# Causal decay attention and two MoE layers on one core: row maxima carried as ten columns

## The chip, the core and the metric

The kernel runs on one core of a Trainium2 chip. The core has five engines with a queue of instructions each: PE (TensorE, the matmuls), DVE (VectorE), ACT (ScalarE), POOL (GpSimd) and SP (SyncE, which here only issues DMAs). Every queue runs in order, so an instruction that waits holds up all that stands behind it. The metric is the device time of one launch in microseconds; less is better.

## What is computed

```python
# 4 batches, 8 heads, 576 positions, 64 per head; all fp32 (weights arrive as float64 and are converted)
scores = q @ k.T / 8 + cum[:, :, :, None] - cum[:, :, None, :]     # cum = cumsum(log(clip(f, 1e-4, 1)))
scores = where(causal, -1e9, scores)
scores = scores - max(scores, axis=-1, keepdims=True)
attn = exp(scores); attn = attn / (sum(attn) + 1e-9)
x = (attn @ v)                                  # 2304 tokens x 512
h = x @ w_in;  x = (max(h, 0) + alpha * min(h, 0)) @ w_out          # 512 -> 2048 -> 512
h = x @ w_in2; out = (h * tanh(softplus(h))) @ w_out2               # 512 -> 2048 -> 512
```

## The kernel before

**Order.** The program is not written in the order in which it runs. Each step is handed to a planner (class `Plan`) with an engine, a cost, a due time `at` and the keys that it reads and writes. The planner lists the steps for every engine by due time and by what is ready in its own estimate, and each engine then runs its list in order. Two tables bend this: `PRIO` adds an offset to the due time of a step, named by stage and number, and `ENG` says which engine takes a step that several could take.

**Attention.** The 32 heads go in 16 pairs, one head on partitions 0 to 63 and one on 64 to 127. A pair passes these stages. `load_qk` and `load_v` bring q, k and v (SP). `load_bias` brings three rows of the decay to KM (for the maxima) and to BK (for the scores); they come from a tensor `biasd`, which the prologue works out from f, and for pair 0 straight from the prologue's tile. `stage_T` casts q and k to QM and KM on ACT. `stage_M` computes the scores once in a single pass, twelve matmuls per pair into the three banks of the group "one" (banks 4 to 6), and one DVE instruction for each (line 623) takes the maxima along keys; they land in the tile M5. Stage `NM2` at its end turns the maxima into rows: M5 holds five chunks of 128 columns, in which two columns carry maxima and the rest is zero, five PE transpositions (line 635) bring them to a bank pair of the group "two" (banks 0 to 3), and two ACT instructions (line 640) copy the result, with a vector `bvec` that adds the constant rows, to BQ. `stage_S` then computes the exact scores in four pieces, each as q times k plus BQ times BK (line 660), and ACT takes the exponential into Pt. POOL masks the diagonal (line 678) and adds up key blocks (line 696). `stage_R` sums over keys on PE (line 708), and ACT and DVE work out the reciprocal in `rr` and `uu`, of which there is one tile each. `stage_V` multiplies Pt by v (line 742), and DVE scales the result by `uu` into X (line 748).

**Keeping PE warm.** Thirty matmuls with the identity run first (line 519), and four follow each matmul of pair 0's `stage_M` and each piece of its `stage_S`. An fp32 matmul shows as two instructions in the trace.

**MoE layers.** Weights come as float64 and are turned to fp32 in halves, by one ACT instruction (line 399) and three DVE ones (lines 401, 403, 405), and then split into a high part (ACT) and a low part (POOL or DVE, line 331). The first four slots of the first layer, eight tiles, are loaded during pairs 0 to 3. `group_a` runs those four slots for three token blocks as a filler between attention's matmuls, and for the other three blocks after attention (`swap1` frees its memory then). `moe_block` runs the rest: `h_mm` (lines 786 to 788), `prelu` or `mish`, `split_g` (high part on ACT, low part by line 331), `out1` (lines 851 to 853) or `out2` (lines 862 to 864). `store_w` converts the second layer's weights during the first and parks them in DRAM.

Of the kernel before, what the change touches and what calls it, by code (L numbers as in the profile page):

```python
# [237 lines left out]
def fox_attention__then__moe_prelu__then__moe_mish(  # L238
# [282 lines left out]
    def prologue():  # L521
# [60 lines left out]
    def load_v(pr, at):  # L582
        plan.stage("LV2")
        i = pr % 2
        n4 = (NQ - 1) * P
        dma(at, lambda: nc.sync.dma_start(vt[i][:, :NQ - 1], v[pr, :n4].rearrange("(c p) x -> p c x", p=P)), 262, runs=1.3, w=[("v", i, 0)])
        dma(at, lambda: nc.sync.dma_start(vt[i][:HALF, NQ - 1], v[pr, n4:]), 33, r=[("vpad", i)], w=[("v", i, 1)], issue=0.62)
# [454 lines left out]
```

## Time and profile before

| | |
|---|---|
| three runs, median (lowest to highest) | 1057.97 us (1057.28 to 1059.17) |
| the profiled execution, its own time | 1058.0 us |
| span of the profile of that execution | 1056.2 us |
| PE busy | 1017.5 us, 96% of the span |
| DVE, ACT, POOL busy | 745.1, 542.1 and 414.2 us |
| granted TensorE clock, mean | 0.994 |
| DMA | 71.06 MB, mean 67 GB/s |

The span is that of the one profiled execution, and 1.8 us of its time lie outside it. The stages follow each other: attention with its filler to about 277 us, the rest of `group_a` to about 360, the first MoE layer to about 620, and the second to the end. A matmul's busy time overlaps that of its neighbours, so a busy PE need not be a PE at its full rate: the count of matmuls in a stretch tells more.

### The profile page before, as it was taken

Reading aid. Unit: us, or ns where it says so; the run is one execution under the profiler, and the core shown is the slowest. Engines: PE = TensorE matmul, PEld = TensorE weight load, DVE = VectorE, ACT = ScalarE, POOL = GpSimd, SP = SyncE. Lnnn points to the kernel's source line nnn. Section 1 sums busy time; section 2 is a strip of 40 time slices with the busy share of each in tenths; the row PEclk is TensorE's granted clock in tenths of the full one; section 3 lists DMA queues with packets and bytes.
Section 4 is the critical chain, followed back from the end, with each engine's and each line's share of the span. In section 5 each row is a group of like instructions: output and inputs, shape, how many; then the busy total and the mean of one; then the engine's idle time right before and its main releaser. Section 6 shows DMA issues by size and latency. Waiting matters only on the chain.

```text
span 1056.2 us, 16992 instructions
## 1 busy us (share of the span) xinstructions
PE 1017.5 (96%) x5996; PEld 914.7 (87%) x5996; DVE 745.1 (71%) x1673; ACT 542.1 (51%) x1133; POOL 414.2 (39%) x423
## 2 busy tenths in 40 slices
PE   7989999999978999999999999999999999999998
PEld 7756677777778999999999999998999989999897
DVE  6587655656588767888612247979888788887885
ACT  4777656664454544444332336555455454554543
POOL 4575543553455562413232324242233322423231
PEclk9999999999999999999999999999999999999999
DMA  5233221210133345565500034100000000000000
GB/s 163 89 110 98 79 70 36 71 48 12 44 117 100 125 137 183 183 207 182 163 1 1 20 92 129 41 1 31 1 6 25 1 30 1 1 31 1 31 1 31
DMA packets 55399, 71.06 MB, mean 67 GB/s; under 512 B 6673, under 2 KB 32273, under 8 KB 55313
## 3 DMA queue, kind: packets, MB, share of 16 engines
q1 hardware_dynamic: 55312, 69.97, 21.2%
q8 instruction: 47, 0.77, 0.3%
q14 instruction: 40, 0.32, 0.1%
HBM read 56.60 MB, written 13.33 MB: 66 GB/s over the span
## 4 chain that ended last, share of the span: by engine, by line
PE 85%; DVE 6%; DMA 3%; ACT 2%; issue 2%; POOL 1%; SPq 0%; ACTq 0%; DVEq 0%; POOLq 0%
PE b L786 12%; PE b L787 11%; PE b L788 11%; PE b L660 6%; PE b L863 6%; PE b L862 6%; PE b L864 6%; PE b L851 5%; PE b L853 5%; PE b L852 5%; PE b L742 4%; PE b L616 3%; PE b L519 2%; DVE wb L403 2%; PE b L708 2%
## 5 line engine op out<-in xcount | busy, mean ns | idle before, releaser
L786 PE MATMUL b<-xh,w 128*128 128x384 f32 x768 | 261.1, 340 | 9.0 <-ACT x L321 5.4
L788 PE MATMUL b<-xl,w 128*128 128x384 f32 x768 | 258.7, 337 | 0.0
L787 PE MATMUL b<-xh,w 128*128 128x384 f32 x768 | 258.6, 337 | 0.0
L843 POOL TENSOR_TENSOR x<-x 128x384 f32<-128x384 f32 x96 | 112.5, 1172 | 246.6 <-DVE x L841 165.7
L786 PEld LDWEIGHTS b<-xh,w 128*128 128x128 f32 x768 | 145.2, 189 | 17.6 <-ACT x L321 6.4
L787 PEld LDWEIGHTS b<-xh,w 128*128 128x128 f32 x768 | 145.2, 189 | 4.0
L788 PEld LDWEIGHTS b<-xl,w 128*128 128x128 f32 x768 | 145.0, 189 | 0.0
L331 POOL TENSOR_TENSOR g<-X,g 128x384 fp32r<-128x384 f32 x72 | 78.6, 1095 | 164.8 <-ACT g L321 128.4
L851 PE MATMUL b<-g,w 128*128 128x384 f32 x384 | 131.8, 343 | 9.4 <-DVE x L811 2.5
L853 PE MATMUL b<-g,w 128*128 128x384 f32 x384 | 129.8, 338 | 0.7 <-POOL g L331 0.6
L852 PE MATMUL b<-g,w 128*128 128x384 f32 x384 | 129.3, 337 | 0.0
L321 ACT CAST g<-x 128x384 fp32r<-128x384 f32 x120 | 61.4, 512 | 115.5 <-POOL x L843 105.0
L864 PE MATMUL b<-w,g 128*128 128x512 f32 x288 | 113.2, 393 | 0.0
L863 PE MATMUL b<-w,g 128*128 128x512 f32 x288 | 113.2, 393 | 0.0
L862 PE MATMUL b<-w,g 128*128 128x512 f32 x288 | 113.1, 393 | 0.0
L811 DVE SCALAR_TENSOR_TENSOR X<-X,alph,b 128x384 f32<-128x384 f32 x72 | 43.9, 611 | 84.3 <-ACT X L805 83.8
L623 DVE CUSTOM_DVE_ANT_0 junk<-b,tri 128x320 f32<-128x320 f32 (+3 forms) x160 | 69.4, 434 | 45.8 <-PE b L616 33.2
L331 DVE TENSOR_TENSOR g<-x,g 128x384 fp32r<-128x384 f32 x102 | 74.9, 736 | 17.6 <-ACT g L321 17.3
L399 ACT ACTIVATE wb<-raw 128x256 f32<-128x256 f32 x128 | 52.2, 432 | 66.8 <-DMA wd<-wb 38.2
L851 PEld LDWEIGHTS b<-g,w 128*128 128x128 f32 x384 | 72.6, 189 | 13.8 <-DVE x L814 3.4
L805 ACT ACTIVATE X<-b 128x384 f32<-128x384 f32 x72 | 35.2, 489 | 88.7 <-PE b L788 88.0
L401 DVE TENSOR_SCALAR wb<-wb 128x256 int32<-128x256 int32 x128 | 55.1, 450 | 33.9 <-ACT wb L399 33.0
(93 smaller groups left out, 1973.7 us busy)
## 6 DMA issues: line engine op xcount, KB each, us to landing
raw<-in_moe_w_in_dram SPq DMA_DIRECT2D x64, 256.0 KB
raw<-in_moe_w_out_dram SPq DMA_DIRECT2D x64, 256.0 KB
wd<-wb SPq DMA_DIRECT2D x32, 256.0 KB
raw<-wd SPq DMA_DIRECT2D x32, 256.0 KB
qt<-in_q_dram SPq DMA_DIRECT2D x16, 288.0 KB
kt<-in_k_dram SPq DMA_DIRECT2D x16, 288.0 KB
out_dram<-x SPq DMA_DIRECT2D x18, 256.0 KB
vt<-in_v_dram SPq DMA_DIRECT2D x16, 256.0 KB
```

What stands on the lines that cost most here:

```text
L331: plan.add(engs, 0.0, at, lambda e: (nc.gpsimd if e == "POOL" else nc.vector).tensor_tensor(out=out(), in0=in0(), in1=in1(), op=ALU.subtra ...
L623: nc.vector.tensor_tensor_reduce(out=junk[ql, :z - a], in0=ps()[ql, :z - a], in1=tri[ql, x0 + a:x0 + z], scale=-1.0, scalar=BIG if n == 0 ...
L786: nc.tensor.matmul(ps[:, :NB], w[:, 0, c], xh[c], start=(c == 0), stop=False)
L787: nc.tensor.matmul(ps[:, :NB], w[:, 1, c], xh[c], start=False, stop=False)
L788: nc.tensor.matmul(ps[:, :NB], w[:, 0, c], xl[c], start=False, stop=(c == KC - 1))
L843: add("POOL", c_pool(NB, 2.2), lambda e, m: nc.gpsimd.tensor_tensor(out=m, in0=e, in1=m, op=ALU.mult), [ek, mk], [mk])
L851: nc.tensor.matmul(ps[:, :NB], w[:, 0, c], g[:, 0], start=first, stop=False)
L852: nc.tensor.matmul(ps[:, :NB], w[:, 1, c], g[:, 0], start=False, stop=False)
L853: nc.tensor.matmul(ps[:, :NB], w[:, 0, c], g[:, 1], start=False, stop=last)
L862: nc.tensor.matmul(ps, g[:, 0, sl], w[:, 0], start=first, stop=False)
L863: nc.tensor.matmul(ps, g[:, 0, sl], w[:, 1], start=False, stop=False)
L864: nc.tensor.matmul(ps, g[:, 1, sl], w[:, 0], start=False, stop=last)
```

## The change

1. **Maxima.** M5 becomes a tile of 128 x 10, one column for each head and chunk. One PE transposition into one bank of the group "one" gives 10 x 128, one copy (ACT by the tables) brings it to a new tile MT, and four DMAs on SP carry the rows of MT to the two rows of BQ. The constant rows of BQ are written once, in the prologue, by POOL. `bvec` goes.
2. **Loads.** v of pair 0 waits for the bias rows of KM. The first weights are loaded for pairs 1 to 4 in place of 0 to 3, all four `w_in` before the four `w_out`, and each load waits for one of the pair's BQ rows (`behind`).
3. **Two buffers** of `rr` and `uu`; the sums of `stage_R` no longer wait for the last use of `uu`.
4. **Tables.** Nearly every offset of `PRIO` is another, and `ENG` has more entries. Against the list of before, 72 subtractions of `split_g` in the first MoE layer go from POOL to DVE, and six copies out of PSUM go from ACT to DVE on balance. All other instructions stay on their engines. Three DVE steps of the prologue are marked `port=BOTH`, which makes the planner keep them clear of POOL's steps in its own estimate. The diff below leaves `PRIO` out, a line of some 2,000 characters; `ENG` is whole.

```diff
-ENG = {('A0g', 0): 'ACT', ('A1g', 0): 'ACT', ('A2g', 3): 'DVE', ('AX', 1): 'DVE', ('AX', 3): 'DVE', ('AX', 5): 'DVE', ('AX', 7): 'DVE', ('B3', 4): 'DVE', ('H0', 4): 'ACT', ('H1', 14): 'DVE', ('O1', 5): 'DVE', ('WF', 2): 'DVE', ('X0', 1): 'POOL', ('X0', 3): 'POOL', ('X0', 7): 'POOL', ('X1', 3): 'POOL', ('X1', 5): 'POOL', ('X1', 7): 'POOL'}
+ENG = {('A0g', 0): 'ACT', ('A0g', 2): 'ACT', ('A0g', 3): 'POOL', ('A1g', 0): 'ACT', ('A2g', 0): 'DVE', ('A2g', 2): 'ACT', ('A2g', 3): 'DVE', ('A3g', 0): 'DVE', ('AX', 1): 'DVE', ('AX', 2): 'ACT', ('AX', 3): 'DVE', ('AX', 4): 'ACT', ('AX', 5): 'DVE', ('AX', 7): 'DVE', ('B0', 4): 'DVE', ('B3', 4): 'DVE', ('H0', 4): 'ACT', ('H0', 7): 'DVE', ('H1', 13): 'ACT', ('H1', 14): 'DVE', ('NM2', 1): 'ACT', ('NM2', 2): 'ACT', ('O1', 3): 'DVE', ('O1', 5): 'ACT', ('R2', 3): 'POOL', ('T2', 2): 'ACT', ('T2', 3): 'ACT', ('WA', 12): 'ACT', ('WA', 13): 'POOL', ('WF', 2): 'DVE', ('X0', 0): 'ACT', ('X0', 1): 'POOL', ('X0', 2): 'ACT', ('X0', 3): 'POOL', ('X0', 4): 'ACT', ('X0', 6): 'ACT', ('X0', 7): 'POOL', ('X1', 0): 'ACT', ('X1', 3): 'POOL', ('X1', 4): 'ACT', ('X1', 5): 'POOL', ('X1', 6): 'ACT', ('X1', 7): 'POOL'}
...
-            half_w(src, kind, fc, i, m, at, after if i else ())
+            half_w(src, kind, fc, i, m, at, [*(after if i else ()), *behind])
...
+    FIRST = [("KMr", 0, e) for e in range(2)]
+    W_FROM = 1
...
-    M5 = [ap1.tile([P, NQ, P], F32, tag=f"M5{i}", name=f"M5{i}") for i in range(2)]
+    M5 = [ap1.tile([P, 2, NQ], F32, tag=f"M5{i}", name=f"M5{i}") for i in range(2)]
+    MT = [ap1.tile([2 * NQ, P], F32R, tag=f"MT{i}", name=f"MT{i}") for i in range(2)]
...
-    rr = ap1.tile([P, S], F32, tag="rr", name="rr")
-    uu = ap1.tile([P, S], F32, tag="uu", name="uu")
+    rrs, uus = ([ap1.tile([P, S], F32, tag=f"{t}{i}", name=f"{t}{i}") for i in range(2)] for t in ("rr", "uu"))
...
-            plan.add("POOL", 0.7, -17 + 9 * i, lambda i=i: G.memset(M5[i], 0.0), w=[("M5", i, c, e) for c in range(NQ) for e in range(2)])
+            plan.add("POOL", 1.2, -17 + 9 * i, lambda i=i: (
+                G.memset(BQ[i].bitcast(F32), 0.0), [G.memset(BQ[i][e * HALF:e * HALF + 3].bitcast(F32), 1.0) for e in range(2)]), w=[("BQ1", i)])
+            plan.add("POOL", 0.2, -17 + 9 * i, lambda i=i: G.memset(M5[i], 0.0), w=[("M5", i, c, e) for c in range(NQ) for e in range(2)])
...
-        ps, bk = plan.use("two")
-        def tr():
-            for c in range(NQ):
-                q0 = rows(c)[0]
-                half = int(q0 >= W0)
-                nc.tensor.transpose(ps()[half][:, q0 - half * W0:q0 - half * W0 + P], M5[i][:, c], ident)
...
-                    nc.scalar.activation(BQ[i][:, a:z], ps()[half][:, :z - a], AF.Identity, bias=bvec)
...
+        ps, bk = plan.use("one")
+        plan.add("PE", 0.11, at + 6, lambda: nc.tensor.transpose(ps()[:2 * NQ, :P], M5[i].rearrange("p e c -> p (e c)"), ident),
+                 ["ident"] + [("M5", i, c, e) for c in range(NQ) for e in range(2)], [bk, ("MT", i)])
+        copy(at + 6.3, P, lambda: MT[i], lambda: ps()[:2 * NQ, :P], [bk], [("MT", i)], ps=True)
+        for e in range(2):
+            for c, n in ((0, 1), (1, NQ - 1)):
+                q0, w = rows(c)
+                dma(at + 6.5, lambda e=e, c=c, n=n, q0=q0, w=w: nc.sync.dma_start(
+                    BQ[i][e * HALF + 1:e * HALF + 2, q0:q0 + n * w].bitcast(F32),
+                    MT[i][e * NQ + c:e * NQ + c + n, :w].bitcast(F32)),
+                    2, r=[("MT", i), ("BQ1", i)], w=[("BQ", i, e, min(c, 1))], issue=0.62)
...
-                if h < 2 * GA:
-                    load_w(0, h % 2, h // 2, h // 2, at + (h % 2) * II + W_AT)
+                h -= 2 * W_FROM
+                if 0 <= h < 2 * GA:
+                    load_w(0, h // GA, h % GA, h % GA, at + (h % 2) * II + W_AT, behind=[("BQ", pr % 2, 0, 0)])
```

**Where the order moves.** First PE, at the place where pair 0's maxima are turned (tile M50) and its scores begin (line 660, tile BQ0); KM1 and QM1 are pair 1, the second use of KM0 and QM0 is pair 2. Before:

```order
L635 MATMUL b0_65<-ident_73,M50_142 128x128 x3
L635 MATMUL b1_66<-ident_73,M50_142 128x128 x2
L616 MATMUL b4_69<-KM1_1_137,QM1_1_133 128x256
L616 MATMUL b5_70<-KM1_0_136,QM1_0_132 128x64
L616 MATMUL b6_71<-KM1_1_137,QM1_1_133 128x64
L660 MATMUL b2_67<-qt0_124,kt0_127 128x288
L660 MATMUL b3_68<-qt0_124,kt0_127 128x288
L660 MATMUL b2_67<-BQ0_140,BK0_138 128x288
```

And now:

```order
L634 MATMUL b4_69<-ident_73,M50_142 10x128
L620 MATMUL b5_70<-KM1_1_137,QM1_1_133 128x256
L620 MATMUL b4_69<-KM1_0_136,QM1_0_132 128x64
L620 MATMUL b6_71<-KM1_1_137,QM1_1_133 128x64
L620 MATMUL b5_70<-KM1_0_136,QM1_0_132 128x448
L620 MATMUL b4_69<-KM1_1_137,QM1_1_133 128x448
L620 MATMUL b6_71<-KM1_0_136,QM1_0_132 128x320
L620 MATMUL b5_70<-KM1_1_137,QM1_1_133 128x320
L620 MATMUL b4_69<-KM1_0_136,QM1_0_132 128x192
L620 MATMUL b6_71<-KM1_1_137,QM1_1_133 128x192
L620 MATMUL b5_70<-KM0_0_134,QM0_0_130 128x320
L620 MATMUL b4_69<-KM0_1_135,QM0_1_131 128x320
```

Three matmuls stood between the transpositions and the first scores; now eleven do, and pair 1's `stage_M` ends before the scores of pair 0 begin (their rows follow).

Second PE, at the turn of pair 2's maxima (M50 again) and its first scores (qt2, kt2, BQ0). Before, one matmul stands between:

```order
L635 MATMUL b2_67<-ident_73,M50_142 128x128 x3
L635 MATMUL b3_68<-ident_73,M50_142 128x128 x2
L616 MATMUL b4_69<-KM1_0_136,QM1_0_132 128x256
L660 MATMUL b2_67<-qt2_126,kt2_129 128x288
L660 MATMUL b3_68<-qt2_126,kt2_129 128x288
```

And now (L708 is `stage_R` and L743 is `stage_V` of pair 0):

```order
L634 MATMUL b6_71<-ident_73,M50_142 10x128
L620 MATMUL b5_70<-KM1_0_136,QM1_0_132 128x320
L708 MATMUL b0_65<-Pt0_122,ones_157 64x128 x2
L708 MATMUL b0_65<-accp_149,ones_157 64x160 x2
L708 MATMUL b1_66<-accp_149,ones_157 64x288 x2
L743 MATMUL b6_71<-Pt0_122,vt0_147 64x320 x6
L743 MATMUL b6_71<-Pt0_122,vt0_147 64x192 x2
L743 MATMUL b6_71<-Pt0_122,vt0_147 64x64 x2
L620 MATMUL b5_70<-KM1_1_137,QM1_1_133 128x320
L620 MATMUL b4_69<-KM1_0_136,QM1_0_132 128x256
L660 MATMUL b2_67<-qt2_126,kt2_129 128x448
L660 MATMUL b3_68<-qt2_126,kt2_129 128x448
```

The sums over keys, a window of `stage_V` and three matmuls of `stage_M` have moved in between.

Third, after attention, the copy of block 3's output out of bank 4 (tile x2_3), which the next block's first matmuls need. Before it is on ACT, behind the conversions of two weights:

```order
L399 ACTIVATE wb0_92<-raw0_91 128x256 x2
L321 CAST w6_0_2651<-wb0_92 128x512
L399 ACTIVATE wb1_2643<-raw1_2642 128x256 x2
L399 ACTIVATE wb0_92<-raw0_91 128x256 x2
L321 COPY x2_3_2639<-b4_69 128x384
```

Now it is on DVE, after the split of the next block's x:

```order
L403 SCALAR_TENSOR_TENSOR wb1_2633<-raw1_2632,wb1_2633 128x256
L405 SCALAR_TENSOR_TENSOR wb1_2633<-raw1_2632,wb1_2633 128x256 x2
L331 TENSOR_TENSOR xl1_101<-X_111,xh1_97 128x384
L331 TENSOR_TENSOR xl2_102<-X_111,xh2_98 128x384
L323 COPY x2_3_2629<-b4_69 128x384
L331 TENSOR_TENSOR xl3_103<-X_111,xh3_99 128x384
```

The copy changes its engine, and no step of a weight that is loaded later stands ahead of it in its new queue.

## Rows read from the trace of the kernel before

**Rows 1.** The page, its first line.

```profile
span 1056.2 us, 16992 instructions
```

**Rows 2.** Busy time by stretch: us, engines with (xcount), PEclk, DMA share, GB/s.

```profile
7.00:28.00 21.00, 21.00 (x171) 20.98 (x172) 11.95 (x45) 10.15 (x19) 4.41 (x11) 1.00 0.51 138
...
40.00:100.00 60.00, 54.30 (x420) 37.49 (x422) 45.67 (x168) 44.81 (x94) 38.34 (x47) 1.00 0.37 115
100.00:277.00 177.00, 171.75 (x1293) 131.22 (x1289) 100.12 (x336) 102.68 (x213) 85.49 (x108) 1.00 0.16 49
277.00:360.00 83.00, 71.13 (x378) 67.20 (x375) 67.99 (x144) 45.25 (x105) 43.11 (x33) 0.96 0.34 108
...
400.00:520.00 120.00, 115.44 (x653) 114.64 (x654) 101.02 (x220) 51.44 (x121) 36.21 (x34) 0.99 0.59 191
520.00:620.00 100.00, 100.00 (x579) 100.00 (x578) 24.48 (x43) 30.14 (x62) 31.83 (x30) 1.00 0.08 22
```

**Rows 3.** Timeline, PE in pair 7: start, us, engine line op, count.

```profile
130.00 0.76 PE L635 MATMUL b<-ident,M 128*128 128x128 f32 x5
130.51 0.42 PE L851 MATMUL b<-g,w 128*128 128x384 f32 x1
```

**Rows 4.** Chain that ended last, two steps of attention: start, us, what.

```profile
118.31 2.21 PE b L742 x20
...
131.40 1.13 PE b L708 x12
```

**Rows 5.** Instructions by line: count | busy us, mean ns | idle before, releasers.

```profile
L331 POOL TENSOR_TENSOR g<-X,g 128x384 fp32r<-128x384 f32 x72 | 78.6, 1095 | 164.8 <-ACT g L321 128.4 <-DVE wb L401 19.8 <-PE b L853 10.0
L331 DVE TENSOR_TENSOR g<-x,g 128x384 fp32r<-128x384 f32 x102 | 74.9, 736 | 17.6 <-ACT g L321 17.3
...
L403 DVE SCALAR_TENSOR_TENSOR wb<-raw,wb 128x256 int32<-128x256 int32 x128 | 63.5, 524 | 0.3
...
L405 DVE SCALAR_TENSOR_TENSOR wb<-raw,wb 128x256 int32<-128x256 int32 x128 | 59.1, 489 | 0.3
...
L401 DVE TENSOR_SCALAR wb<-wb 128x256 int32<-128x256 int32 x128 | 55.1, 450 | 33.9 <-ACT wb L399 33.0
...
L640 ACT ACTIVATE BQ<-b,bvec 128x320 fp32r<-128x320 f32 (+1 forms) x32 | 14.2, 494 | 8.6 <-PE b L635 8.5
```

**Rows 6.** Chain that ended last, pair 3's load of k.

```profile
46.41 3.47 DMA kt<-in_k_dram
```

**Rows 7.** Tile KM: small DMA issues on SP, duration ns min/median/max.

```profile
L579 SPq DMA_DIRECT2D KM<-biasd x30: 231/255/274, 16.7 to 222.4; - x30
```

**Rows 8.** Waits of PE's weight loads, 40 to 277 us: total, times, longest.

```profile
PEld b L616 <- DVE M L623: 7.5, 18, 1.0
```

**Rows 9.** Timeline, PE at the start.

```profile
6.92 8.48 PE L519 MATMUL b<-ident 128*128 128x128 f32 x60 [6.92 <-POOL ident masks.py:199]
15.16 0.39 PE L616 MATMUL b<-KM,QM 128*128 128x320 f32 x1
...
30.04 0.76 PE L660 MATMUL b<-qt,kt 64*128 64x288 f32 x4
```

**Rows 10.** Timeline, PE after attention.

```profile
281.12 0.44 PE L786 MATMUL b<-xh,w 128*128 128x384 f32 x1 [1.45 <-DVE X L748]
...
300.58 0.69 PE L786 MATMUL b<-xh,w 128*128 128x384 f32 x1 [4.07 <-ACT x L321]
301.07 0.52 PE L787 MATMUL b<-xh,w 128*128 128x384 f32 x1
301.39 0.52 PE L788 MATMUL b<-xl,w 128*128 128x384 f32 x1
```

**Rows 11.** Timeline, ACT and POOL at the same place.

```profile
299.42 0.75 ACT L399 ACTIVATE wb<-raw 128x256 f32<-128x256 f32 x2 [2.99 <-POOL w L331]
300.07 0.46 ACT L321 COPY x<-b 128x384 f32<-128x384 f32 x1
...
291.20 1.29 POOL L331 TENSOR_TENSOR w<-wb,w 128x512 fp32r<-128x512 f32 x1
295.86 3.53 POOL L331 TENSOR_TENSOR w<-wb,w 128x512 fp32r<-128x512 f32 x1 [3.37 <-ACT w L321]
```

More of the change, by code (lines that the diff above doesn't have):

```diff
@@ L406, in half_w, with conv_w @@
             out=wb(), in0=half(0, I32), scalar=29, in1=wb(), op0=ALU.logical_shift_right, op1=ALU.bitwise_or), [rwk, wbk], [wbk], port=BOTH)
-    def conv_w(l, kind, fc, at, after=()):
+    def conv_w(l, kind, fc, at, after=(), behind=()):
         src = ((w_in1, w_out1), (w_in2, w_out2))[l][kind]
@@ L421, in split_w, with load_w @@
         minus(at, DM, lambda: wslot[w][:, 1], bf, lambda: wslot[w][:, 0].bitcast(F32), wbk + [hk], [lk])
-    def load_w(l, kind, fc, slot, at, after=()):
+    def load_w(l, kind, fc, slot, at, after=(), behind=()):
         plan.stage("W" if after else "WA")
-        split_w(*conv_w(l, kind, fc, at, after), (slot, kind), at, after)
+        split_w(*conv_w(l, kind, fc, at, after, behind), (slot, kind), at, after)
     wd = {}
@@ L531, in prologue @@
         plan.add("POOL", 0.6, -12, lambda: G.memset(bias[:, 1], 1.0), r=pk, w=["bias1"])
-        plan.add("DVE", 0.5, -9, lambda: V.tensor_scalar(fr, fr, 1e-4, 1.0, op0=ALU.max, op1=ALU.min), ["f"] + pk, ["f1"])
+        plan.add("DVE", 0.5, -9, lambda: V.tensor_scalar(fr, fr, 1e-4, 1.0, op0=ALU.max, op1=ALU.min), ["f"] + pk, ["f1"], port=BOTH)
         plan.add("ACT", 0.67, -9, lambda: nc.scalar.activation(fr, fr, AF.Ln), ["f1"] + pk, ["f2"])
         plan.add("DVE", 0.8, -9, lambda: V.tensor_tensor_scan(
-            out=cum, data0=fr, data1=tri[:NH, :S], initial=0.0, op0=ALU.add, op1=ALU.add), ["f2", "zero"] + pk, ["cum"])
+            out=cum, data0=fr, data1=tri[:NH, :S], initial=0.0, op0=ALU.add, op1=ALU.add), ["f2", "zero"] + pk, ["cum"], port=BOTH)
         m8 = -(float(D) ** 0.5)
@@ L538, in prologue @@
         plan.add("DVE", 0.75, -9, lambda: V.scalar_tensor_tensor(
-            out=bias[:, 2].bitcast(F32R), in0=cum, scalar=m8, in1=bias[:, 0], op0=ALU.mult, op1=ALU.subtract), ["bh", "cum"] + pk, ["bl"])
-        plan.add("DVE", 0.5, -20, lambda: (V.memset(bvec, 0.0), [V.memset(bvec[e * HALF:e * HALF + 3], 1.0) for e in range(2)]), w=["bvec"])
+            out=bias[:, 2].bitcast(F32R), in0=cum, scalar=m8, in1=bias[:, 0], op0=ALU.mult, op1=ALU.subtract), ["bh", "cum"] + pk, ["bl"], port=BOTH)
         plan.add("POOL", 0.3, -10, lambda: (G.memset(ones, 1.0), G.memset(eps, 1e-9)), w=["ones"])
@@ L584, in load_v @@
         i = pr % 2
+        after = FIRST if pr == 0 else []
         n4 = (NQ - 1) * P
[L586 to L587 removed]
+        dma(at, lambda: nc.sync.dma_start(vt[i][:, :NQ - 1], v[pr, :n4].rearrange("(c p) x -> p c x", p=P)), 262, runs=1.3, r=after, w=[("v", i, 0)])
+        dma(at, lambda: nc.sync.dma_start(vt[i][:HALF, NQ - 1], v[pr, n4:]), 33, r=[("vpad", i)] + after, w=[("v", i, 1)], issue=0.62)
     def stage_T(pr, at):
@@ L708, in mm @@
                     nc.tensor.matmul(ps()[half][hs[e], a - half * h2:z - half * h2], ones, src, start=True, stop=True)
-        plan.add("PE", 4 * S / 2.4e3 + 0.02, at + 4, mm, ["acc", "ones"] + p_keys(i, [0]), [bk, "uu"] + [("rr", x) for x in range(2)], mode="c")
+        plan.add("PE", 4 * S / 2.4e3 + 0.02, at + 4, mm, ["acc", "ones"] + p_keys(i, [0]), [bk], mode="c")
         V = nc.vector
@@ L749, in stage_V @@
                 out=dst, in0=ps()[:, :z - a0], scalar=-1.0, in1=uu[:, a0:z], op0=ALU.mult, op1=ALU.mult),
-                [bk, "uu"], [("X", b, hh + e, n) for e in range(2)])
+                [bk, ("uu", i)], [("X", b, hh + e, n) for e in range(2)])
     load_qk(0, -12)
```

27 lines of the change are left out of this document (10 added, 17 removed).

## The prediction

> **What bounds the kernel now.** I read the stretches first [rows 2]. From 100 to 277 us, where attention runs with its filler, PE is idle for 177 - 171.75 = 5.3 us, while DVE works 57% of the time, ACT 58% and POOL 48%: PE is the bound there, and an instruction taken from it is worth its time. From 40 to 100 us PE is idle for 5.7 of 60 us and DVE works 76%; PE's weight loads wait most often for the maxima on DVE, 7.5 us in 18 waits over both stretches [rows 8], and the chain passes through a load of k for 3.47 us [rows 6]. That stretch is bound by PE in part only. From 7 to 28 us PE never pauses, because the identity matmuls fill it [rows 2, 9]. After attention I count matmuls. In a steady stretch one starts every 0.173 us (100 us for 579, [rows 2]). From 277 to 360 us there are 378, worth 65.4 of 83 us, so 17.6 us are lost; from 400 to 520 us 653, worth 113.0 of 120, so 7.0 are lost. Part of the first loss has an address: PE waits 1.45 us for the last X and 4.07 us for a copy out of PSUM [rows 10]. Of the clock the rows say that it is granted whole in attention and 0.96 from 277 to 360 [rows 2]; after the wait of 4.07 us matmuls start every 0.32 us [rows 10], about half the rate of the steady stretch, which is the lower of the two levels (1.2 and 2.4 GHz).
>
> **The sum, part by part,** against the profiled execution's own 1058.0 us (span 1056.2 [rows 1], 1.8 us around it); the median of the three runs is 1057.97, so the two bases agree.
>
> *Transpositions.* Five take PE from 130.00 to 130.51 us [rows 3], 0.10 us each; one remains, and a pair saves 0.41 us. In the eleven pairs that are turned after 100 us PE is the bound, which makes -4.5 us. For the first five I count nothing, since other waits end last there. Bounds: 0 and 16 x 0.41 = -6.6. The transposition moves from the bank pairs of the scores to the three banks of the maxima; it holds one of them for the copy's time, in exchange for a pair, and I count that at zero: the three banks turn over twelve times per pair anyway. That cover is gone where a maximum already ends last [rows 8].
>
> *Copies.* ACT loses 14.2 us of BQ copies [rows 5] and gets 16 of a 10 x 128 tile, each between 0 and 0.44 us (14.2/32). ACT is 58% busy in that stretch [rows 2], so nothing on the path: 0.
>
> *Rows by DMA, the new wait.* BQ is ready after the copy (up to 0.44 us), four issues (0.26 us each by the nearest small one [rows 7], 1.02 together) and the landing. No row shows a small DMA's landing. It lies between 0 and the 3.47 us of the 288 KB load of k [rows 6], a small DMA being between no transfer and that one; I take the middle, 1.7, so 3.2 us in all (0.44 + 1.02 + 1.7), with bounds of 1.5 and 4.9. Against it stands what PE now does between the transposition and the first matmul that reads BQ. For pair 2 that is the sums (1.13 us), ten matmuls of `stage_V`, 20 instructions (2.21 us) [rows 4], and three maxima matmuls of some 0.2 us: 3.9 us. Before, one matmul stood there. For pairs 0, 1 and 3 eight to eleven matmuls of the maxima stand there, each held to DVE's pace. So it is covered by 0.7 us. I take +0.5 us in all for pairs where SP comes late: SP runs in order, BQ's rows stand behind loads of q, k and weights that wait for a free tile, and whatever waits in front of them delays PE. At the upper bound pair after pair waits 1.0 us, 16 x 1.0 = +16. The 64 issues are 16 us on a queue that mostly sleeps: 0.
>
> *Start.* The identity stands two clears earlier on POOL, so the thirty warm matmuls, which begin at 6.92 us and end as the first maxima matmul starts at 15.16 [rows 9], may end earlier. That matmul also needs the bias rows, and their DVE chain now stands behind three more clears and their ACT step behind seven casts in place of three; I count no gain. The scores of pair 0, at 30.04 us before [rows 9], now stand behind all of pair 1's maxima, about 4 us later; pair 1's are then done, and by the turn of pair 2 PE has the same rows behind it. Taken as +0.5, bounds -2 and +4.
>
> *First weights one pair later.* Before, three of the eight tiles are converted before pair 0's sums; now none is. Each takes DVE 2 x (0.450 + 0.524 + 0.489) = 2.9 us [rows 5], so 8.8 us move into 40 to 100 us, where DVE has 60 - 45.7 = 14.3 us free [rows 2]. What goes into a free slot costs nothing, what stands in front of a maximum costs its time. I take +1, bounds 0 and 8.8. Loads of v behind the bias rows: v is not needed before pair 0's `stage_V`, 0.
>
> *Two buffers* of reciprocals: no wait of PE for `uu` shows among its waits in attention; 0, or a few tenths gained.
>
> *After attention.* Bank 4, for which PE waits at 281.12, is in the new order last used by pair 14, whose reciprocals are done early: -1.45. The copy for which PE waits 4.07 us ran at 300.07 on ACT, behind a conversion that waited 2.99 us for a POOL subtraction of 3.53 us, against 1.29 us for one like it [rows 11]; it is now on DVE, behind nothing that waits for that subtraction. With the wait goes the slow stretch behind it, nine matmuls at 0.32 for 0.173 us: 4.07 + 1.3 = 5.4. Of the 6.9 us I take 5.5, since the next block's split and the next raw weights are then close behind. The rest of the two losses, 17.6 - 6.9 + 7.0 = 17.7 us, I leave as it is; half of it could go or come with a new order, -9 to +6.
>
> Sum: -4.5 + 0.5 + 0.5 + 1 - 5.5 = -8.0, so 1050.0 us; its own range is 1044 to 1055.
>
> **A rule against the change.** For the nearest load the row shows 3.47 us from issue to use [rows 6], and none shows whether a small one is as slow. The Trainium skill, "DMA: Bandwidth & Descriptors", section "Rules for kernel authors", says that transfers below 64 KB are mostly overhead and should be joined into one, and its section "Anatomy of one DMA" gives about 2 us of fixed cost for a DMA of the GpSimd path; this is 64 such transfers on SP. By it the new chain would be 0.44 + 1.02 + 2.0 = 3.5 us and its cover 0.4 us in place of 0.7: if SP is late by half a microsecond in half of the pairs, that is 8 x 0.1 = 0.8 us more. No run here shows it yet.
>
> **Rivals.**
> (a) *The rows land late; slower.* It decides when copy, issues and landing pass 3.9 us in most pairs: then the scores wait every time. If SP stands still another 1 us per pair on a load in front of BQ's rows, and the landing is at its upper bound, a pair waits 1 + 1 = 2 us, 32 us in all: 1050 + 32 = 1082. Gains are gone at 0.5 us per pair (8.0/16). For it: four in-order issues on a queue with waiting loads. Against: the order puts 3.9 us of work or more in between.
> (b) *DVE takes over; slower by a little.* 8.8 us of conversions in 40 to 100 us at the full price, and 72 subtractions that go from POOL to DVE in the first MoE layer. At 0.736 us [rows 5] they add 53 us; some 33 fall into 400 to 520 us, 24 us on top of 101.0 of 120 [rows 2], 5 us too many unless the second layer's conversions slip into 520 to 620, where DVE has 75 us free. 1050 + 7.8 + 5 = 1063. Against: they can slip.
> The subtraction of 3.53 us beside one of 1.29 [rows 11] shows POOL held up while DVE works. The Trainium skill, "SBUF — State Buffer", section "Who interferes with whom", says that a DVE instruction with two SBUF inputs and a GpSimd instruction that reads SBUF lock each other out; by that rule the 78.6 us that leave POOL [rows 5] also stop holding DVE, and (b) would cost less than it says.
> (c) *New stalls after attention for the old.* The 5.5 us come back at another copy or weight: 1055.5 to 1058, say 1057, no change.
> (d) *Attention is not PE's.* PE's work shrinks, and the maxima end last: 5.5 us gained after attention less 2 lost to the other terms: 1054.5.
> (e) *The new order clears more.* Half of the 17.7 us goes as well: 1041.
>
> **Chances.** Forecast 0.47, (a) 0.10, (b) 0.06, (c) 0.12, (d) 0.12, (e) 0.13. A run of this kernel can tell 0.2% from no change, about 2.1 us: faster is below 1055.9. Forecast, (d) and (e) are faster, 0.72; (c) is the same, 0.12; (a) and (b) are slower, 0.16. The range of 1037 to 1062 leaves out (a) and the far end of (e).
>
> **What would show it.** The copies to MT and the first matmul on BQ give each pair's chain: right if PE's waits for a BQ DMA are below 2 us in all, wrong and (a) if above 8. Right on the transpositions if 100 to 277 us shrinks to some 172 us for the same work. (b) shows as DVE above 90% in 400 to 520 us with PE waiting for it; (c) as waits of PE of 4 us or more between the last X and 80 us later. The prediction is wrong from the ground up if PE waits more in attention than before.

## The result, and the profile after

| | before | after |
|---|---|---|
| median (lowest to highest) | 1057.62 us (1056.53 to 1059.17, 4 runs) | 1044.01 us (1039.91 to 1045.40, 4 runs) |
| ratio to before, 95% interval | | 0.9864 (0.9833 to 0.9895) |
| the profiled execution, its span | 1058.0, 1056.2 us | 1039.9, 1038.2 us |

The change takes 13.6 us off, where 8.0 were forecast; the time lies in the range, at the very edge of the forecast's own 1044 to 1055. The profiled execution of after is the fastest of the four, 4 us under the median, so its trace is read for places and not for the last microseconds. Two executions of the same instructions differ, too: the kernel before and the one with 72 subtractions moved (below) are the same up to the end of attention, and the next stage begins at 277.29 us in one and at 279.10 in the other.

These are the stretches of after that answer to [rows 2]: us, PE, PEld, DVE, ACT, POOL with (xcount), granted clock, DMA share, GB/s. The first line is of before, whose stretch from 28 to 40 us those rows leave out.

```profile
28.00:40.00 12.00, 11.40 (x86) 8.85 (x84) 6.97 (x29) 6.89 (x16) 5.21 (x6) 1.00 0.20 52
```

```profile
28.00:40.00 12.00, 10.18 (x42) 6.57 (x43) 5.73 (x26) 1.34 (x3) 0.65 (x2) 0.72 0.01 4
40.00:100.00 60.00, 53.95 (x361) 36.00 (x361) 39.65 (x145) 37.81 (x83) 36.31 (x42) 0.89 0.35 110
100.00:277.00 177.00, 172.70 (x1301) 128.64 (x1299) 111.47 (x374) 103.67 (x223) 95.78 (x117) 1.00 0.21 63
277.00:360.00 83.00, 79.87 (x469) 77.30 (x466) 69.91 (x150) 44.13 (x102) 37.40 (x29) 1.00 0.33 105
360.00:400.00 40.00, 39.99 (x231) 39.67 (x230) 35.28 (x82) 22.05 (x52) 14.94 (x11) 1.00 0.41 131
400.00:520.00 120.00, 120.00 (x695) 120.00 (x694) 93.63 (x246) 52.66 (x122) 6.15 (x6) 1.00 0.63 200
```

Attention gained nothing in all. Its end on PE is told by the first matmul of the fourth token block (block 3), before which all of PE's work for attention and the whole filler, 288 matmuls of the first MoE layer, have begun; before and then after:

```profile
277.29 0.45 PE L786 MATMUL b<-xh,w 128*128 128x384 f32 x1
```

```profile
279.52 0.44 PE L787 MATMUL b<-xh,w 128*128 128x384 f32 x1
```

It comes 2.2 us later, hardly more than the 1.8 us by which those two executions differ. The loss lies in the first pairs: pair 3's maxima are turned at 73.20 us, before at 65.81. From there on the changed kernel wins back 5 us, about what fewer transpositions were to save, but its order on PE is another, so this doesn't show that they are the cause. The clock, whole in this part of before, is 0.72 from 28 to 40 us and 0.89 from 40 to 100. After 277 us the new kernel runs away: 469 matmuls against 378 up to 360 us, 695 against 653 from 400 to 520. Of the first layer's matmuls 1647 have begun by 520 us, against 1544; 103 more, at 0.173 us, are 17.8 us.

PE's longest waits in after behind that for the identity at the start, total, times, longest, where before had the 4.07 us of [rows 10]:

```profile
PE b L620 <- DVE M L627: 3.1, 10, 0.4
PE b L620 <- DVE nmx L627: 2.6, 3, 1.7
PE b L634 <- DVE nmx L627: 2.5, 2, 2.1
PE b L660 <- ACT Pt L669: 1.2, 1, 1.2
PE b L852 <- DVE x L815: 1.2, 1, 1.2
PE b L854 <- POOL g L331: 1.1, 1, 1.1
```

The first four lie in attention, and three of them are waits for maxima on DVE. After attention none is longer than 1.2 us. No wait for one of BQ's DMAs is among them.

### The profile page after: what moved, and what is told of

The parts are those of the page before. It is cut to its first block, busy times and chain, and to the rows that moved or that the text cites. A ratio compares the mean times of both kernels' runs of the same rounds, so it can differ in the third digit from the quotient of the medians.

```text
span 1038.2 us, 16819 instructions
## 1 busy us (share of the span) xinstructions
PE 1013.0 (98%) x5932; PEld 906.8 (87%) x5932; DVE 746.0 (72%) x1748; ACT 527.6 (51%) x1111; POOL 341.4 (33%) x357
## 4 chain that ended last, share of the span: by engine, by line
PE 89%; DVE 6%; ACT 2%; issue 1%; POOL 1%; DMA 0%; DVEq 0%; SPq 0%; POOLq 0%
PE b L787 12%; PE b L788 12%; PE b L789 12%; PE b L865 6%; PE b L864 6%; PE b L863 6%; PE b L660 6%; PE b L852 6%; PE b L854 6%; PE b L853 6%; PE b L743 3%; PE b L620 3%; PE b L521 2%; DVE junk L627 2%; PE b L708 1%
## 5 line engine op out<-in xcount | busy, mean ns | idle before, releaser
L852 PE MATMUL b<-g,w 128*128 128x384 f32 x384 | 129.7, 338 | 1.2 <-DVE x L815 1.2
L854 PE MATMUL b<-g,w 128*128 128x384 f32 x384 | 128.7, 335 | 1.4 <-POOL g L331 1.1
L853 PE MATMUL b<-g,w 128*128 128x384 f32 x384 | 128.4, 334 | 0.0
L331 DVE TENSOR_TENSOR g<-x,g 128x384 fp32r<-128x384 f32 x102 | 69.9, 686 | 42.8 <-ACT g L321 42.8
L669 ACT ACTIVATE Pt<-b 128x512 f32<-128x512 f32 (+1 forms) x128 | 56.5, 501 | 47.0 <-PE b L660 44.0
L331 POOL TENSOR_TENSOR xl<-X,xh 128x384 fp32r<-128x384 f32 x18 | 19.1, 1069 | 173.3 <-ACT xh L321 172.9
L836 ACT ACTIVATE x<-x,two 128x384 f32<-128x384 f32 x96 | 58.6, 613 | 33.5 <-DVE x L834 33.0
```

Of the source, the lines that this page charges most:

```text
L331: plan.add(engs, 0.0, at, lambda e: (nc.gpsimd if e == "POOL" else nc.vector).tensor_tensor(out=out(), in0=in0(), in1=in1(), op=ALU.subtra ...
L852: nc.tensor.matmul(ps[:, :NB], w[:, 0, c], g[:, 0], start=first, stop=False)
L853: nc.tensor.matmul(ps[:, :NB], w[:, 1, c], g[:, 0], start=False, stop=False)
L854: nc.tensor.matmul(ps[:, :NB], w[:, 0, c], g[:, 1], start=False, stop=last)
```

## Experiments

All kernels are compared with the kernel before on the same chip. Differences between two of them are taken from the medians; two intervals that overlap are told as such. The medians of the kernel before in these comparisons lie between 1057.1 and 1058.0 us, so a difference between kernels of two comparisons is uncertain by up to 0.9 us from that alone.

### Tables or code

The kernel before with the two tables of after, and the reverse:

```diff
-PRIO = PRIO_OF_THIS
-ENG = ENG_OF_THIS
+PRIO = PRIO_OF_THE_OTHER
+ENG = ENG_OF_THE_OTHER
```

> The kernel before with the changed kernel's PRIO and ENG and nothing else. Theory O (the order brought it): up to 277 us the two traces have done the same 292 matmuls of the first MoE layer, and the whole difference opens between 277 and 520 us, where only the order changed; then this kernel takes 1042 to 1050 us, and PE's wait of 4.07 us for a copy of x after attention is gone. Rival C (the code of attention and of the loads brought it, and the later stages only follow from it): 1054 us or more.

Measured: 1040.81 us, ratio 0.9844 (0.9822 to 0.9866). The tables alone do it all, a little more than theory O's range had; theory O holds. That both traces have the same matmuls of the first layer by 277 us proves nothing, though: 288 are all that the filler has, so the count stops there.

> The changed kernel with the PRIO and ENG of before. Theory O: the losses after 277 us come back, 1054 to 1064 us. Rival C: the code alone carries the gain, 1042 to 1050 us.

Measured: 1068.35 us, ratio 1.0114 (1.0092 to 1.0135). It is slower than before, and by more than theory O had: under the old tables the changed code costs 11 us, under the new ones 1044.0 - 1040.8 = 3, where the two intervals overlap. So the code loses something, clearly under the old tables, and the tables win more than the result shows.

Next, before with the new entries of the MoE stages alone:

> The kernel before with the changed PRIO and ENG for the stages of the MoE layers only (A0 to X1, W, WF, WS, H and O); the entries of attention, of its loads and of the first weights (WA) are those of before. The kernel before with all of the new tables took 1040.8 us. Theory O2 (the gain lies in the order of the MoE stages): 1040 to 1046. Rival T (the entries of attention carry half of it or more): 1049 to 1058.

Measured: 1037.88 us, ratio 0.9810 (0.9789 to 0.9830), 20.1 us less than before, and more than theory O2's range had. The gain lies in the entries of the MoE stages, which hold offsets and engines; for the code of before, the new entries of attention even seem to cost 2.9 us (the two intervals overlap a little).

### Two pieces of the tables, each by itself

For these two the order was kept as the planner had made it, and only the engine of the named steps was changed when they were emitted (`FORCE` overrides the planner's engine):

```diff
+FORCE = {('B0', 4): 'DVE'}
...
-            fn = lambda f=f: f(e)
+            fn = lambda f=f: f(FORCE.get(key, e))
```

> The kernel before in an unchanged order, with only the six copies of the first output chunk of each token block (stage B0, group_a) on DVE in place of ACT. Theory of the forecast: PE's wait of 4.07 us at 300.58 us and the slow stretch behind it go, -5.4 us, 1051.5 to 1053.5. Rival N (the next copy, split or weight is late at once and takes its place): 1056 to 1058.5.

Measured: 1055.38 us, ratio 0.9975 (0.9965 to 0.9984): 2.6 us, half of the forecast and in neither theory's range. The copy no longer stands behind ACT's conversions, and is late all the same. DVE and then PE at that place in this kernel:

```profile
297.57 1.81 DVE L403 SCALAR_TENSOR_TENSOR wb<-raw,wb 128x256 int32<-128x256 int32 x2
299.31 0.55 DVE L323 COPY x<-b 128x384 f32<-128x384 f32 x1
```

```profile
299.90 0.45 PE L786 MATMUL b<-xh,w 128*128 128x384 f32 x1 [2.65 <-DVE x L323]
```

Two steps of a conversion stand in front of it and take 1.81 us beside a subtraction on POOL that runs from 296.56 to 299.10 us, where two take 0.74 us at 294.41; PE still waits 2.65 us. With all of the new tables this wait is gone: PE's waits for such a copy in the trace of after are 0.6 us at most.

The second piece has `FORCE = {('H0', 7): 'DVE'}`, the 72 subtractions:

> The kernel before in an unchanged order, with only the 72 low parts of split_g in the first MoE layer on DVE in place of POOL. Rival (b) of the prediction: DVE has 24 us more in 400 to 520 us than it has room for by 5 us, so 1059 to 1063. Theory G (in before these subtractions on POOL, 1.1 us each and held up by DVE, are what the second matmul group waits for): the 7 us lost between 400 and 520 us come back at least in half, 1050 to 1054. Neither: 1056.5 to 1058.5.

Measured: 1053.80 us, ratio 0.9958 (0.9942 to 0.9974), 4.2 us less. Rival (b) had the sign wrong. The groups of before from 400 to 520 us, count, busy us and mean ns:

```profile
L403 DVE SCALAR_TENSOR_TENSOR wb<-raw,wb 128x256 int32<-128x256 int32 x60 | 33.6, 582 | 0.3
L331 POOL TENSOR_TENSOR g<-X,g 128x384 fp32r<-128x384 f32 x28 | 30.0, 1074 | 85.5 <-ACT g L321 54.8 <-DVE wb L401 19.8 <-PE b L853 7.4
L405 DVE SCALAR_TENSOR_TENSOR wb<-raw,wb 128x256 int32<-128x256 int32 x59 | 26.3, 470 | 0.3
L401 DVE TENSOR_SCALAR wb<-wb 128x256 int32<-128x256 int32 x58 | 24.4, 430 | 11.1 <-ACT wb L399 10.5
```

The same with the subtractions on DVE, and the stretch as a whole:

```profile
L403 DVE SCALAR_TENSOR_TENSOR wb<-raw,wb 128x256 int32<-128x256 int32 x60 | 24.3, 426 | 0.3
L405 DVE SCALAR_TENSOR_TENSOR wb<-raw,wb 128x256 int32<-128x256 int32 x60 | 23.6, 417 | 0.3
L331 DVE TENSOR_TENSOR g<-X,g 128x384 fp32r<-128x384 f32 x29 | 16.6, 577 | 0.2 <-ACT g L321 0.2
L401 DVE TENSOR_SCALAR wb<-wb 128x256 int32<-128x256 int32 x56 | 16.3, 299 | 12.8 <-ACT wb L399 12.7
```

```profile
400.00:520.00 120.00, 120.00 (x694) 120.00 (x694) 95.29 (x249) 51.75 (x122) 6.42 (x6) 1.00 0.63 198
```

DVE got 29 more instructions and is busy for 95.3 us in place of 101.0. Its conversions had been held up by POOL's subtractions, and run at 426, 417 and 299 ns in place of 582, 470 and 430. PE makes 694 matmuls in place of 653: the 7 us lost in this stretch are all back. The total gains less; in this execution block 3 begins at 279.10 us, 1.8 us later than in before, though the instructions up to there are the same. PE's waits of before in this stretch show that it did not stand for a subtraction on POOL itself:

```profile
PE b L851 <- ACT g L321: 2.2, 1, 2.2
PE b L851 <- DVE x L905: 1.3, 1, 1.3
PE b L851 <- ACT wb L399: 1.1, 1, 1.1
```

With the subtractions on DVE none of the three is left. One meeting of the two engines in before, DVE and then POOL:

```profile
411.46 1.10 DVE L401 TENSOR_SCALAR wb<-wb 128x256 int32<-128x256 int32 x1
```

```profile
411.19 1.22 POOL L331 TENSOR_TENSOR g<-X,g 128x384 fp32r<-128x384 f32 x1 [7.69 <-DVE wb L401]
```

The DVE step, 0.29 us at 410.80, ends 0.15 us after POOL's: it took 0.81 us more. The Trainium skill, "SBUF — State Buffer", section "Who interferes with whom", names such a lock between DVE and GpSimd, over a pair of ports that they share; the trace agrees, and it gives the size. For a DVE step with one SBUF input, as this one, the section has the lock in a mode with two ports alone, and no row shows the mode.

### The transposition

```diff
-lambda: nc.tensor.transpose(ps()[:2 * NQ, :P], ..., ident),
+lambda: [nc.tensor.transpose(ps()[:2 * NQ, :P], ..., ident) for _ in range(NQ)],
```

> The changed kernel with each pair's 10 x 128 transposition made five times, in an unchanged order: 64 more PE matmuls of about 0.10 us, 0.41 us a pair. Theory P (PE sets the end of attention, as the forecast's -4.5 us supposed): 4 to 6.6 us more than the changed kernel's 1044, so 1048 to 1051. Rival D (another engine's work or the clock sets it): at most 1.5 us more, 1044 to 1045.5; the extra matmuls could even keep the clock up and make it 1 us less.

Measured: 1044.61 us, ratio 0.9880 (0.9862 to 0.9898): 0.6 us by the medians, and the intervals overlap. That is what rival D had; but the change's own four times spread over 5.5 us, so a cost of some 4 us can't be shut out, and that PE's time for transpositions is free here is not shown. Its stretches from 28 to 100 us:

```profile
28.00:40.00 12.00, 10.33 (x39) 6.63 (x39) 5.43 (x24) 1.34 (x3) 0.65 (x2) 0.72 0.02 4
40.00:100.00 60.00, 53.32 (x392) 35.34 (x394) 43.43 (x150) 39.47 (x88) 34.88 (x43) 1.00 0.35 110
```

The granted clock from 40 to 100 us is 1.00, where the changed kernel's profile has 0.89. That fits extra matmuls paid back by the clock. The mean clock of the whole launch goes the same way in every execution, 0.993 to 0.996 here and 0.986 to 0.990 in the changed kernel; what of the time it pays back is not shown.

The same edit on the changed kernel with the loads as before (the next section):

> The changed kernel with the loads as before (1035.3 us) and each pair's 10 x 128 transposition made five times, in an unchanged order; 64 more PE matmuls of 0.10 us, 6.6 us in all, 4.5 of them in pairs turned after 100 us. The code without the loads gains 5.6 us under the new tables (1040.8 to 1035.3). Theory P2 (that gain is PE's time for transpositions, which the late weights hid in the changed kernel): 1038.5 to 1042. Rival D2 (PE's time still isn't it; the freed bank pair, the two buffers or ACT's shorter copies are): 1034 to 1037.

Measured: 1039.50 us, ratio 0.9833 (0.9818 to 0.9848), against 1035.25 and 0.9780 (0.9758 to 0.9802) without it. Here the extra matmuls cost 4.2 us by the medians and 5.6 by the ratios, and the intervals are apart. Theory P2 holds: the saving is there. That the changed kernel hides it is likely and no more, by the spread above.

### The loads

```diff
-    FIRST = [("KMr", 0, e) for e in range(2)]
-    W_FROM = 1
+    FIRST = []
+    W_FROM = 0
...
-    load_v(0, 2)
+    load_v(0, -1)
...
-                    load_w(0, h // GA, h % GA, h % GA, at + (h % 2) * II + W_AT, behind=[("BQ", pr % 2, 0, 0)])
+                    load_w(0, h % 2, h // 2, h // 2, at + (h % 2) * II + W_AT)
```

> The changed kernel with the loads as before: v of pair 0 without its wait, first weights from pair 0 on, in the old order, without a wait for BQ's rows. The changed code cost 3 us under the new tables (1044.0 against 1040.8) and 11 under the old (1068.4 against 1057.1). Theory W (the weights one pair later cost it: their conversions on DVE, 2.65 us for two at 69.4 us, stand in front of pair 3's maxima and PE waits 2.14 us there): 1040 to 1042, and pair 3's transposition near 70 us as in the kernel before with the new tables. Rival Q (the columns and the rows by DMA cost it): 1043 to 1046.

Measured: 1035.25 us (1031.71 to 1036.49), ratio 0.9780 (0.9758 to 0.9802). It is 8.8 us faster than the whole change, with the edit above as its only difference, and no kernel here is faster; theory W had the direction and less than half of the size. Its stretches:

```profile
28.00:40.00 12.00, 10.21 (x54) 7.18 (x54) 7.35 (x35) 3.98 (x11) 3.20 (x4) 0.86 0.21 66
40.00:100.00 60.00, 56.34 (x437) 38.01 (x433) 44.74 (x157) 43.01 (x92) 40.25 (x48) 1.00 0.36 108
277.00:360.00 83.00, 82.01 (x466) 80.30 (x465) 69.08 (x163) 48.80 (x112) 40.54 (x30) 1.00 0.37 115
```

From 40 to 100 us PE makes 437 matmuls where the changed kernel makes 361, at a full clock in place of 0.89. Pair 3's maxima are turned at 65.57 us in place of 73.20, and block 3 begins at 273.36 us in place of 279.52:

```profile
65.57 0.28 PE L634 MATMUL b<-ident,M 128*10 128x128 f32 x1 [0.18 <-DVE nmx L627]
273.36 0.44 PE L787 MATMUL b<-xh,w 128*128 128x384 f32 x1
```

How DVE's work lay in the changed kernel is seen in 8 us steps:

```profile
40.00:48.00 8.00, 7.62 (x54) 5.51 (x54) 3.09 (x13) 3.08 (x8) 5.17 (x6) 1.00 0.38 122
48.00:56.00 8.00, 7.94 (x79) 5.43 (x75) 4.04 (x16) 7.22 (x17) 3.32 (x6) 1.00 0.38 126
...
64.00:72.00 8.00, 6.83 (x56) 4.45 (x52) 7.57 (x23) 4.98 (x11) 5.80 (x6) 1.00 0.44 143
72.00:80.00 8.00, 6.02 (x24) 3.80 (x24) 7.03 (x29) 3.77 (x8) 4.24 (x4) 0.71 0.35 105
```

DVE has half of its time free from 40 to 56 us and next to none from 64 to 80, where the late conversions meet the maxima of pair 3. A full DVE is not the harm by itself; with the old loads the same stretches are as full, and PE keeps its pace, since pair 3's maxima are nearly done when they begin:

```profile
64.00:72.00 8.00, 7.22 (x61) 4.34 (x57) 6.98 (x26) 6.00 (x13) 7.00 (x7) 1.00 0.48 145
72.00:80.00 8.00, 7.69 (x69) 4.91 (x65) 7.36 (x26) 5.46 (x14) 2.26 (x4) 1.00 0.39 117
```

The worst of it in the changed kernel, DVE, POOL and PE:

```profile
69.42 2.65 DVE L403 SCALAR_TENSOR_TENSOR wb<-raw,wb 128x256 int32<-128x256 int32 x2
```

```profile
69.28 2.16 POOL L696 TENSOR_TENSOR accp<-Pt 128x896 f32<-128x896 f32 x1 [0.90 <-POOL Pt L677]
```

```profile
73.20 0.27 PE L634 MATMUL b<-ident,M 128*10 128x128 f32 x1 [2.14 <-DVE nmx L627]
```

A conversion, held up by POOL's sum over key blocks, stands in front of a maximum, and PE waits 2.14 us. In the stretch in which that wait ends the clock is 0.71.

Is it the later pairs or the wait? The next kernel keeps the later pairs and their new order, and takes only the waits away (`behind` and `FIRST`, and v's due time):

```diff
-    FIRST = [("KMr", 0, e) for e in range(2)]
+    FIRST = []
...
-                    load_w(0, ..., behind=[("BQ", pr % 2, 0, 0)])
+                    load_w(0, ...)
```

> The changed kernel with the first weights still for pairs 1 to 4 and in the new order, but without their wait for BQ's rows, and v of pair 0 without its wait. In DVE's order the first conversion then stands at place 14, as with the loads as before, and not at place 83. Old loads gave 1035.3, the change 1044.0. Theory W1 (one pair later by due time costs it, since more conversions stand among the maxima of pairs 3 to 6): 1041 to 1044. Rival W2 (the wait for the rows costs it, since it empties DVE in pairs 0 and 1 and fills it later): 1034.5 to 1038.

Measured: 1048.53 us, ratio 0.9917 (0.9903 to 0.9931), slower than the changed kernel by 4.5 us and beyond W1's own range. The wait does not cost; without it the later weights cost more. So the cost comes with the later pairs or with the new order among the weights, which no run here takes apart. Why it is more without the wait is open: the trace has the clock at 0.57 from 28 to 40 us and 0.89 from 40 to 100, and PE behind ACT's exponentials at 61.20 us, but the planner made another order for it.

### Start, buffers, and the entries of attention

Two identity matmuls behind each of pair 1's maxima, in an unchanged order:

```diff
-                        if pr == 0:
-                            warm(KEEP)
+                        if pr <= 1:
+                            warm(KEEP if pr == 0 else 2)
```

> The changed kernel with two identity matmuls behind each of pair 1's twelve maxima matmuls, in an unchanged order. In the trace of after the granted clock is 0.74, 0.50, 0.50 and 0.55 in the four stretches from 30 to 38 us, where PE works 1.5 to 2 of each 2 us, waiting for DVE's maxima, and the first scores start at 34.55 us at half rate. Theory K (the fallen clock is what the start loses): the clock stays at 1.0 from 28 to 40 us, the third piece of the scores comes 1.5 to 3 us earlier, and the time is 1041 to 1042.5 us. Rival M (the maxima on DVE set the pace there): 1043.5 to 1045.

Measured: 1040.86 us, ratio 0.9849 (0.9831 to 0.9868). The interval overlaps that of the change, so the total is unclear. Its stretches:

```profile
32.00:36.00 4.00, 4.00 (x35) 3.42 (x34) 2.87 (x14) 0.14 (x1) 0.00 (x0) 1.00 0.02 4
36.00:40.00 4.00, 4.00 (x32) 3.07 (x31) 0.78 (x3) 1.79 (x5) 0.66 (x2) 1.00 0.00 0
...
56.00:64.00 8.00, 7.60 (x31) 5.15 (x31) 6.16 (x24) 4.89 (x11) 5.57 (x8) 0.54 0.16 46
```

The clock stays whole to 40 us and pair 2's maxima are turned 1.7 us earlier (50.60 against 52.31). By pair 3 the lead is gone (74.21 against 73.20); the clock is 0.54 from 56 to 64 us, where the changed kernel has 0.79. What the start gains is lost again by pair 3 in this execution; whether the 3.2 us by the medians are real is open.

One tile each of `rr` and `uu`, and then the old entries of attention, both on the kernel with the old loads:

```diff
-    rrs, uus = ([ap1.tile(...) for i in range(2)] for t in ("rr", "uu"))
+    rrs, uus = ([ap1.tile(...) for i in range(1)] * 2 for t in ("rr", "uu"))
```

> The changed kernel with the loads as before (1035.3 us) and one tile each of rr and uu, in an unchanged order. Forecast's term: 0 or a few tenths, 1034 to 1036.5. Rival U (the two buffers carry the 5.6 us): 1038.5 to 1042, with PE waiting for the sums' bank or for X.

Measured: 1035.43 us, ratio 0.9802 (0.9781 to 0.9823), against 0.9780: no difference that these runs can tell. The two buffers are not what carries the code's gain.

> The changed kernel with the loads as before (1035.3 us), and the PRIO and ENG entries of attention and of the first weights as before; the entries of the MoE stages are the new ones. With the code of before, the old entries of attention were 2.9 us better than the new ones (1037.9 against 1040.8). Theory A (they are better here too): 1031 to 1034. Rival B (the new entries fit the steps of the new code, as those of the maxima and of the rows): 1036 to 1043.

Measured: 1035.64 us, ratio 0.9795 (0.9781 to 0.9808), no difference either, and between the ranges of the two theories. The new entries of attention make no difference to the new code that these runs can tell.

## Why the prediction was right in the sum and wrong in its parts

A path from before to after by medians: the MoE entries -20.1 (1037.9), the attention entries +2.9 (1040.8), the code without its loads -5.5 (1035.3), the loads +8.8 (1044.0). That is -13.9, against -13.6 measured. The forecast had the signs of the large parts, and two of its sizes were far off in opposite directions: the loads at 8.8 in place of 1 and the stages after attention at 20.1 in place of 5.5. That the two misses cancelled each other far enough for the sum to stay in its range is luck.

**Transpositions, -4.5.** The size was right: 4.2 us by the run with the old loads. In the changed kernel itself the medians show no more than 0.6 us for 64 more, with a spread that hides a few. Attention as a whole gained nothing, which is rival (d)'s outcome: PE's longest waits there are for maxima, as (d) had it, but (d) didn't name the late conversions in front of them and the fallen clock. The test that I had set, 100 to 277 us shrunk to 172, failed. So did the one that was to show the prediction wrong from the ground up: PE's waits inside attention, added over their lines, rose from 8.0 to 10.8 us. By that sign its picture of attention was wrong, though its total was not.

**Copies, 0.** No matmul waits for a copy to MT, and PE's weight loads wait 0.7 us for it in all; its 16 take 0.25 us each. Not tested apart.

**Rows by DMA, +0.5.** Right in outcome: PE waits for none of them. The issue was mis-sized. The issues of after, and SP's queue at pair 2:

```profile
L640 SPq DMA_DIRECT2D BQ<-MT x64: 518/590/1537, 28.3 to 260.9; - x64
```

```profile
53.78 1.23 SPq L640 DMA_DIRECT2D BQ<-MT  x2
55.09 0.39 SPq L389 DMA_DIRECT2D raw<-in_moe_w_in_dram  x1
55.54 1.18 SPq L640 DMA_DIRECT2D BQ<-MT  x2
```

PE at the same place:

```profile
58.10 0.46 PE L620 MATMUL b<-KM,QM 128*128 128x256 f32 x1 [1.72 <-DVE nmx L627]
58.49 1.87 PE L660 MATMUL b<-qt,kt 64*128 64x448 f32 x4
59.47 1.26 PE L660 MATMUL b<-BQ,BK 64*128 64x448 f32 x2
```

An issue takes 0.59 us and not the 0.26 of the nearest small one [rows 7], so four take 2.4 us and not 1.0. The chain to the last issue of pair 2 lasts from 52.31 to 56.72 us, more than the 3.9 us that were to cover it; PE reads BQ there at 59.47 us, after a wait of 1.72 us for a maximum. That the rows came in time for this pair is in part owed to that wait; how much slack is left was not tried, and the landing shows in no row.

**Start, +0.5.** The scores of pair 0 moved from 30.04 to 34.55 us, as the order had said. The clock's fall to 0.72 was not foreseen. Pair 2 is turned at 52.31 us, before at 52.49, so by then the term was about 0.

**Weights later, +1, bounds 0 and 8.8.** This is the first step that failed; 8.8 us were measured. That this is also the upper bound is chance: the bound was the conversions' own busy time, and the cost came by waits in front of maxima and a lower clock. The step was "DVE has 14.3 us free from 40 to 100 us". The mean over 60 us hid that the free time lies where the moved work isn't: 40 to 56 us is half empty, 64 to 80 full, and there pair 3's maxima stand behind it. The price of a tile, taken from means, also left out that a conversion beside POOL can take 2.65 us for two steps in place of 0.74. And the clock there is 0.71, 0.87 and 0.86 in the stretches from 72 to 100 us, where with the old loads it is whole; no term had that. The stretches are of one execution each, the 8.8 us of the medians.

**Two buffers, 0.** Right as far as the runs can tell.

**After attention, -5.5 and "the rest I leave as it is".** This is the second step that failed, in the other direction: the MoE entries are worth 20.1 us, and nearly all of the 24.6 us of losses that I had counted went. The two waits behind the named 5.5 are gone in the trace of after but for 0.6 us, as forecast; but the copy on DVE alone, in the order of before, gives 2.6, for the wait moved behind a conversion held up by POOL. The largest piece that was found is one that I had priced as a loss: the 72 subtractions, +5 in rival (b), -4.2 measured. There the step was to add 53 us of DVE work to DVE's old durations (and 33 of the subtractions to a stretch in which the row shows 28), though the subtraction of 3.53 us beside one of 1.29 in [rows 11] had already shown the two engines in each other's way. The sentence on the shared ports behind rival (b) said that it would cost less; it went below nothing. Some 13 us of the 20 are not taken apart further. They come with the other MoE entries, the offsets and some engines of copies; which of them is open.

**Rivals.** (a) no wait for rows. (b) the wrong sign; DVE is busy 93.6 of 120 us from 400 to 520. (c) no wait over 1.2 us after attention. (d) the outcome in attention. (e) the outcome after it, and more than its half.

## What to carry to other kernels

Free time of an engine is worth something only where the moved work lands: read it in stretches as short as the loop's own step, not as a mean over the stage, and look which waiting step the moved work will stand in front of. Before pricing work that moves between two engines that hold each other up, ask what the rest of their work gains; here DVE was busy for less time with more to do. When a change has several parts, run it without each: this one was 8.8 us faster without one of its own.

## What the runs showed of the hardware that was not expected

- Conversions on DVE lose to POOL's subtractions: 582, 470 and 430 ns a step beside them, 426, 417 and 299 ns without them.
- A DMA that carries a row between two SBUF tiles takes 0.59 us to issue on SP; on the same queue the small ones from DRAM take 0.26 us.
- 64 more matmuls on PE cost 4.2 us in the kernel with the old loads, where the clock from 40 to 100 us is 1.00 without them and 0.94 with them, and 0.6 us by the medians, within their spread, in the changed kernel, where it is 0.89 without and 1.00 with them.
